# Choosing pages from the first six chunks without a margin in a gated scan with top-1 experts

## The chip, the cores and the metric

The kernel runs on one core of a Trainium2 chip. The metric is device microseconds of one execution; the median of three runs stands for a kernel.

## The reference

```python
def _attn_ref(x, r_gate, i_gate, a_param):          # x: 4 x 5056 x 256
    a_base = sigmoid(a_param)
    a_t = exp(8.0 * sigmoid(r_gate) * log(clip(a_base, 1e-6, 1 - 1e-6)))
    x_gated = sqrt(max(1 - a_t * a_t, 1e-6)) * sigmoid(i_gate) * x
    for t in range(S):
        h = a_t[:, t] * h + x_gated[:, t]
        y[:, t] = h
    return y

def _moe_ref(x, modality_id, w_gate, modality_bias, w1, w2):   # x: 20224 x 256
    logits = x @ w_gate + modality_bias[modality_id]            # 8 experts
    e_idx = argmax(logits); gate_w = softmax(logits)[e_idx]
    for e in range(8):
        mask = e_idx == e
        out[mask] = gate_w[mask] * (relu(x[mask] @ w1[e]) @ w2[e])   # w1: 256x1024, w2: 1024x256
```

A gated linear recurrence runs over 5,056 steps of four sequences; every token of its output goes to one of eight experts and through that expert's two layers. There are two modalities, each with a bias over the experts, and mostly the bias decides: two experts get nearly all tokens.

## The kernel before, in words

**Chunks.** The scan runs over 23 chunks of time steps: four of 128 steps (512 tokens, as there are four sequences), 17 of 256 (1,024 tokens), one of 128 and one of 64. A chunk is loaded, gated and scanned (L513 to L549), scaled and split into two f16 parts (L663, L666), multiplied by the gate weights (L679), and routed (L738 to L806): each token gets its expert and its place behind the tokens that this expert already has. The chunk's tokens are transposed into rows (`rt`) and an indirect DMA of GpSimd scatters them, 128 at a time, into the buffer `rows` in DRAM (L813), which has a region of `NCAP` rows for each expert. Routing also keeps the running count of every expert, `be`, and after chunk c the counts of the two most frequent experts in units of 256 rows, `b2` (L800).

**Pages.** A page is a run of rows of one expert that TensorE takes through both layers. The two frequent experts (`HOT` = 2) have their weights in SBUF throughout, and their pages come in pairs, one for each. `u` holds, in units of 256 rows, where the next page of each begins. `choose_two` (L913 to L929) computes on VectorE the first rows of the next pair (`sel`) and moves `u` on; `load_rows` on SyncE reads `sel` into a register and loads the page as a transposing DMA (`X`, L1091). TensorE does layer 1 (L1166; pages of 512 rows use a scheme with seven products, L1256) and layer 2 (L1326); ScalarE and VectorE evacuate layer 1 (L1103, L1105), ScalarE layer 2 (L1117), and GpSimd scatters 128 output rows at a time (L1121).

**How much may be chosen.** The program is fixed when it is built, while the counts are only known when it runs. So the number and the sizes of the pages are fixed by a planner: when `have` tokens are routed, a pair of `size` rows each is written into the program if `have - 2 * behind(have)` is at least `chosen + 2 * size`, where `behind(n)` = 1.2 sqrt(n) + 8 is a margin for an expert with fewer tokens than half. `enough` gives the time at which the next pair may be chosen. The first pair has 128 rows each, the others 256, and 512 once the sums for the seven products are ready. Where at run time an expert has too few new rows for a page that was planned, its `sel` points at the null page (empty rows), the page is computed for nothing, and `u` stays.

**The end.** After the last chunk the loop stops when the margin allows no further pair; one more pair of 256 is chosen, whose rows may run out (256 empty rows lie behind each expert's last one). Then come two pages of 128 rows that load and convert weights of their own (`cold_weights`: L384 loads 1 MB for each layer into `cr`, L297 takes squares, L285 to L291 make a scale, L347, L350 and L353 convert): `other`, for the rare expert with the most tokens, and `last`, for the expert, frequent or rare, with the most tokens still left. What remains is for a branch:

```python
def more_pages(n, left):
    with tc.If(nc.values_load(tiles["over"], min_val=0, max_val=N) >= 1):
        ...
        add(choose_more(min(n, left)), (0, 4))     # n pages of 128, weights loaded for each
        ...
        if left > n:
            more_pages(3 * n, left - n)
more_pages(2, (N + E * (P - 1)) // P)
```

`over` is the largest number of tokens that an expert has left. The body computes 2 pages of 128 rows, a nested branch 6, the next 18, and so on; each page goes to the expert with the most tokens left, and has its weights loaded and converted as above.

**Order.** The whole program is written by a planner: generators ask for an engine with a duration, and their instructions are emitted in the order of planned times. Waits at run time are by data and buffers. The four `wr` buffers hold the raw and converted weights of one such page; `X` has four buffers, `po` two.

Of the kernel before, what the change touches and what calls it, by code (L numbers as in the profile page):

```python
# [9 lines left out]
F32 = mybir.dt.float32  # L10
# [4 lines left out]
ALU = mybir.AluOpType  # L15
AX = mybir.AxisListType

P = 128
B, S, D, E, FF = 4, 5056, 256, 8, 1024
# [3 lines left out]
WIDE = 512  # L23
NCAP = N + 256
NULLS = E * NCAP
# [4 lines left out]
CHUNKS = [(128 * k, 128) for k in range(4)] + [(512 + 256 * k, 256) for k in range(17)] + [(4864, 128), (4992, 64)]  # L30
# [4 lines left out]
HOT = 2  # L35
# [11 lines left out]
C_STEP = 2  # L47
URGENT = 0.5
HURRY = 5
ROW_STEP = 2.4  # L50
LAG = 3.0


def behind(n):

    return 1.2 * n ** 0.5 + 8


def columns(c):
# [4 lines left out]
def parts(c):  # L64

    return -(-columns(c) // PART)
# [11 lines left out]
def kernel(  # L78
# [13 lines left out]
    nc = tc.nc  # L92
    pool = lambda name, bufs, **k: ctx.enter_context(tc.tile_pool(name=name, bufs=bufs, **k))
    const = pool("const", 1)
    pa = pool("pa", 2)
    sm = pool("sm", 2)
# [30 lines left out]
    for e in range(E):  # L127
# [23 lines left out]
        out=cmp, in0=rank.rearrange("p e o -> p o e").broadcast_to(one8), in1=ids.broadcast_to(one8), op=ALU.is_equal  # L151
# [7 lines left out]

    u = const.tile([1, HOT], F32, name="u")  # L160
    nc.vector.tensor_scalar(out=u, in0=key[:, 0:HOT, 0], scalar1=NCAP / 256.0, scalar2=None, op0=ALU.mult)
    cold = const.tile([1, E], F32, name="cold")
    nc.vector.tensor_scalar(out=cold, in0=ev, scalar1=HOT - 0.5, scalar2=8.0, op0=ALU.is_ge, op1=ALU.mult)

# [16 lines left out]
        out=um1, in_=um1, pattern=[[1, P]], base=0, channel_multiplier=-1,  # L181
# [33 lines left out]
    plan = {"end": 0.0}  # L215
# [474 lines left out]
    def rows_part(c, j):  # L690
# [34 lines left out]
        for u in range(k):  # L725
            yield "POOL", ROW_STEP if c > 7 else 1.3, None
            scatter(f"rows{c}", rt[:, u, 0:ROW], di[:, PART * j + u : PART * j + u + 1])
# [84 lines left out]
    def scatter(group, src, idx):  # L812
        ins = nc.gpsimd.indirect_dma_start(  # L813
            out=rows[:, :], out_offset=bass.IndirectOffsetOnAxis(ap=idx, axis=0),
            in_=src, in_offset=None, bounds_check=NULLS + WIDE - 1, oob_is_err=False,
        ).ins
        for gname in written:
            tc.declare_no_dep(ins, group=gname, reason="every token has a row of its own")
        tc.declare_no_dep(ins, group="loads", reason="a page's rows are written before it is chosen")
        if group not in written:  # L820
            written.append(group)
        puts.append((group, ins.name))
        tc.add_to_no_dep_group(group, ins)
        free["DMA"] = max(free["DMA"], plan["end"] - 1.3) + 0.37
        if "pe" in count:

            tc.add_manual_dep(
                ins, count["pe"], mybir.DependencyInfo(mybir.DependencyClass.Sync, mybir.DependencyReason.DATA)
            )
# [7 lines left out]
    def null_rows():  # L837

        for k in range(2):
# [3 lines left out]
            for e in range(E):  # L843
                yield "POOL", ROW_STEP, None
                scatter("rows_null", nt, ni[:, e : e + 1])
# [13 lines left out]
    pages, queue = [], []  # L859
    count = {"chosen": 0, "ended": False, "cold": 0, "rows": 0}  # L860
# [3 lines left out]
    def routed(t=FAR):  # L864
        n = 0
        while n < NC and all(mark.get(("put", n, j), FAR) <= t for j in range(parts(n))):
            n += 1
        return n

    def enough():  # L870

        at, have = 0.0, 0
        want = count["chosen"] + HOT * (256 if pages else P)
        for c in range(NC):
            at = max([at] + [mark.get(("put", c, j), FAR) for j in range(parts(c))])
            if at >= FAR:
                return FAR
            have += B * CHUNKS[c][1]
            if have - HOT * behind(have) >= want:
                return at  # L880
        return at

    def new_page(size, e, sel, col, late):
        pg = Page()
        pg.size, pg.st, pg.e, pg.sel, pg.col, pg.routed, pg.late = size, size, e, sel, col, routed(plan["end"]), late
        return pg
# [8 lines left out]
    def new_sel():  # L895
        n = count["sel"] = count.get("sel", 0) + 1
        ticket = take("sel")
        return sm.tile([1, 2], I32, name=f"sel{n}", tag="sel", bufs=BUFS["sel"]), ticket
# [4 lines left out]
        if not left:  # L903
            give("sel", ticket)

    def choose_two(size, full):

        sel, ticket = new_sel()
        b2 = tiles["b2", routed(plan["end"]) - 1]
        z = size / 256  # L910
        if full:
            d = sm.tile([1, HOT], F32, name=f"d{len(pages)}", tag="d2")
            nc.vector.tensor_tensor(out=d, in0=b2, in1=u, op=ALU.subtract)  # L913
            yield "DVE", 0.08, None, 0.0
            nc.vector.tensor_scalar(out=d, in0=d, scalar1=z, scalar2=float(NULLS), op0=ALU.is_lt, op1=ALU.mult)
            yield "DVE", 0.08, None, 0.0
            nc.vector.scalar_tensor_tensor(out=sel, in0=u, scalar=256.0, in1=d, op0=ALU.mult, op1=ALU.max)
            first = plan["end"]
            yield "DVE", 0.08, None, 0.0
            if z == 1:  # L920
                nc.vector.scalar_tensor_tensor(out=u, in0=d, scalar=0.0, in1=u, op0=ALU.is_equal, op1=ALU.add)
            else:
                nc.vector.tensor_scalar(out=d, in0=d, scalar1=0.0, scalar2=z, op0=ALU.is_equal, op1=ALU.mult)
                yield "DVE", 0.08, None, 0.0
                nc.vector.tensor_tensor(out=u, in0=u, in1=d, op=ALU.add)
        else:
            nc.vector.tensor_scalar(out=sel, in0=u, scalar1=256.0, scalar2=None, op0=ALU.mult)
            yield "DVE", 0.08, None, 0.0
            nc.vector.scalar_tensor_tensor(out=u, in0=u, scalar=z, in1=b2, op0=ALU.add, op1=ALU.min)  # L929
        left = [0] * HOT  # L930
        for e in range(HOT):
            pg = new_page(size, e, sel, e, not full)
            pg.ticket = ticket, left
            queue_page(pg)
        count["chosen"] += HOT * size
# [51 lines left out]
    def choose_pages():  # L987
        other, at = None, FAR
        summed = lambda: max(mark.get(("sw", e), FAR) for e in range(HOT))
        look = lambda: drained(count["chosen"] - (LOOK if summed() >= FAR else LOOK_END))()  # L990
        while True:
            yield "DVE", 0.08, allof(enough, room("sel"), look)
            if other is None and routed(plan["end"]) == NC:

                add(null_rows(), (0, 5), plan["end"])
                other, at = (yield from choose_cold(True)), len(pages) + 2 * HOT
                add(cold_weights(other), (1, 3), plan["end"])
                yield "DVE", 0.08, room("sel")
            if len(pages) >= at:
                queue_page(other)  # L1000
                at = FAR
            have = sum(B * t for _, t in CHUNKS[: routed(plan["end"])])
            size = 256 if pages else P
            if summed() <= plan["end"] and have - HOT * behind(have) >= count["chosen"] + HOT * WIDE:
                size = WIDE
            if have - HOT * behind(have) < count["chosen"] + HOT * size:
                break
            yield from choose_two(size, True)
        yield "DVE", 0.08, allof(room("sel"), look, seen("null"))
        yield from choose_two(256, False)  # L1010
        if at < FAR:
            queue_page(other)

        t = sm.tile([1, HOT, E], F32, name="thot", tag="thot", bufs=1)
        yield "DVE", 0.08, None, 0.0
        for r in range(HOT):
            nc.vector.tensor_scalar(out=t[:, r], in0=hm[:, r], scalar1=u[:, r : r + 1], scalar2=65536.0, op0=ALU.mult, op1=ALU.mult)
        for r in range(HOT):
            nc.vector.tensor_tensor(out=tk, in0=tk, in1=t[:, r], op=ALU.max)

        yield "DVE", 0.08, room("sel")
        last = yield from choose_cold(False)
        queue_page(last)
        add(cold_weights(last), (1, 3), plan["end"])
        tiles["over"] = over()
        count["ended"] = True
# [342 lines left out]
    def start_chunk(c):  # L1369
        at = PRIO.get(c, (9 + C_STEP * c, 10 + C_STEP * c, 11 + C_STEP * c, 10 + C_STEP * c))  # L1370
        add(load_chunk(c), (0, 10 + C_STEP * c))
        add(scan_chunk(c), (0, at[2]), urgent=c < HURRY)
        add(size_chunk(c), (0, at[2]), urgent=c < HURRY)
        add(split_chunk(c), (0, at[1]), urgent=c < HURRY)
        add(route_chunk(c), (0, at[0]), urgent=c < HURRY)
        for j in range(parts(c)):
            add(rows_part(c, j), (1, at[3]), urgent=c < HURRY)

# [83 lines left out]
```

## Time and profile before

| | |
|---|---|
| median of three runs | 952.21 us (950.91 to 956.86) |
| the profiled execution | 952.39 us, its span 950.5 us |
| mean granted TensorE clock | 0.978 |
| TensorE, matmul | 869.7 us busy, 8,462 instructions |
| VectorE | 700.0 us |
| ScalarE | 671.6 us |
| GpSimd | 484.7 us |

Engines are PE (TensorE; PEld its weight loads, PEq its sequencer), DVE (VectorE), ACT (ScalarE), POOL (GpSimd) and SP (SyncE); a q behind the name is the engine's queue of instructions that aren't counted as busy. A row of a group names the line, engine, operation, tiles and shapes, the count, then busy us and mean ns of one, and idle time before it with what ended it. In the timeline and the chain the first number is the start in us from the span's beginning, the second the duration. In the slices each digit is the busy share of 1/40 of the span in tenths.

### The profile page before, as it was taken

The page shows a single profiled execution, that of the slowest core. Times are in us where ns is not written, and L with a number is a line of the kernel's source. Part 1 is how long each engine was busy: PE and PEld are TensorE (multiplying, and loading weights), DVE is VectorE, ACT ScalarE, POOL GpSimd, SP SyncE. Part 2 cuts the span into 40 slices and gives each one's busy share as a digit, 9 for nine tenths or more (in the row PEclk, how much of TensorE's full clock was granted, in tenths as well). Part 3 has the DMA queues.
Part 4 walks back from the last instruction along what each step waited for, and adds up shares of the span by engine and source line. Part 5 has one row for each costly group of instructions (what it writes and reads, how often), then busy time and mean ns, then how long its engine had stood idle before and what let it go on. Part 6 is the DMA issues. An engine that isn't in the chain of part 4 may idle for free.

```text
span 950.5 us, 22224 instructions
## 1 busy us (share of the span) xinstructions
PE 869.7 (91%) x8462; PEld 775.0 (82%) x8462; DVE 700.0 (74%) x1535; ACT 671.6 (71%) x960; POOL 484.7 (51%) x506
## 2 busy tenths in 40 slices
PE   2268995879999999999999999999999999999996
PEld 1256884769898888888888888988888888888886
DVE  4977785788888877799886888976886666645551
ACT  6876795866898778889578789844765555554742
POOL 5232456367876758857776658745544221222122
PEclk9988997989999999999999999999999999999999
DMA  8746896759999799987788988685733322213410
GB/s 292 230 150 175 223 244 166 223 135 221 267 203 228 226 256 232 265 224 195 185 217 185 274 208 214 163 161 119 184 79 85 57 62 51 52 45 68 131 36 24
DMA packets 222759, 160.43 MB, mean 169 GB/s; under 512 B 197297, under 2 KB 201522, under 8 KB 216114
## 3 DMA queue, kind: packets, MB, share of 16 engines
q1 hardware_dynamic: 205714, 114.49, 51.2%
q0 software_dynamic: 16224, 44.25, 14.2%
q8 instruction: 68, 1.11, 0.5%
q14 instruction: 49, 0.40, 0.1%
q10 hardware_dynamic: 704, 0.18, 0.1%
HBM read 72.96 MB, written 44.48 MB: 124 GB/s over the span
## 4 chain that ended last, share of the span: by engine, by line
PE 46%; issue 21%; DVE 11%; DMA 8%; POOL 7%; ACT 6%; POOLq 0%; SPq 0%; ACTq 0%; DVEq 0%
PE po L1326 21%; PE ph L1166 21%; POOL out_dram L1121 5%; DMA rows<-rt,di 3%; DVE x L546 3%; DVE H L1105 2%; DMA X<-rows 2%; DMA rt<-a 2%; POOL rows L813 1%; PE pb L1256 1%; DVE x L531 1%; ACT H L1103 1%; PE psl L679 1%; PE pa L1256 1%; DVE g L517 1%
## 5 line engine op out<-in xcount | busy, mean ns | idle before, releaser
L1166 PE MATMUL ph<-X,hw 128*128 128x256 f16 (+1 forms) x2688 | 332.1, 276 | 27.3 <-DMA X<-rows 27.3
L1326 PE MATMUL po<-hw,H 128*128 128x256 f16 x2640 | 328.1, 274 | 2.9 <-DVE H L1105 2.7
L1121 POOL DMA_INDIRECT out_dram<-ot,mt x160 | 195.3, 1221 | 259.7 <-ACT ot L1117 217.9
L813 POOL DMA_INDIRECT rows<-rt,di x158 | 229.4, 1452 | 173.3 <-issue 40.7
L1166 PEld LDWEIGHTS <-hw 128*128 128x128 f16 x2688 | 261.3, 100 | 59.5 <-DMA X<-rows 21.3
L1326 PEld LDWEIGHTS <-H 128*128 128x128 f16 x2688 | 259.5, 98 | 35.0 <-DVE H L1105 3.5
L1105 DVE SCALAR_TENSOR_TENSOR H<-ph,H 128x512 f16<-128x512 f32 (+1 forms) x232 | 151.8, 665 | 80.0 <-ACT H L1103 79.6
L1103 ACT ACTIVATE H<-ph 128x512 f16<-128x512 f32 (+1 forms) x232 | 133.2, 578 | 99.9 <-PE ph L1166 88.1
L1117 ACT ACTIVATE ot<-po,gt 128x256 f32<-128x256 f32 x160 | 75.2, 471 | 50.5 <-PE po L1326 43.5
L546 DVE TENSOR_TENSOR_SCAN x<-a,x 128x2048 f32<-128x2048 f32 (+2 forms) x23 | 88.1, 3829 | 0.8
L1326 PE MATMUL po<-hw,Hx 128*128 128x256 f16 x576 | 81.8, 273 | 0.1
L1326 PE MATMUL po<-hw,Hg 128*128 128x256 f16 x576 | 80.2, 273 | 0.0
L1326 PEld LDWEIGHTS <-Hx 128*128 128x128 f16 x576 | 56.2, 98 | 6.7 <-issue 0.3
L1326 PEld LDWEIGHTS <-Hg 128*128 128x128 f16 x576 | 56.4, 98 | 6.5
L1256 PEld LDWEIGHTS <-sw 128*128 128x128 f16 x576 | 56.4, 98 | 6.5
L531 DVE TENSOR_TENSOR x<-g,x 128x2048 f32<-128x2048 f32 (+2 forms) x23 | 45.8, 1991 | 15.8 <-ACT x L529 15.8
L663 ACT ACTIVATE a<-x,scy 128x1024 f16<-128x1024 f32 (+2 forms) x46 | 45.8, 1021 | 12.3 <-DVE scy L289 12.3
L666 DVE SCALAR_TENSOR_TENSOR a<-x,scy,a 128x1024 f16<-128x1024 f32 (+2 forms) x46 | 50.8, 1122 | 1.7 <-ACT a L663 1.7
L522 ACT ACTIVATE a<-a,ch 128x1024 f32<-128x1024 f32 (+2 forms) x46 | 50.7, 1118 | 0.0
L1103 ACT ACTIVATE Hg<-sv 128x512 f16<-128x512 f32 x48 | 30.0, 627 | 26.5 <-DVE sv L1204 26.2
L517 DVE SCALAR_TENSOR_TENSOR g<-g,x 128x2048 f32<-128x2048 f32 (+2 forms) x23 | 45.6, 1984 | 2.9 <-ACT g L513 2.9
L1199 ACT ACTIVATE sv<-pb 128x512 f32<-128x512 f32 x48 | 28.6, 595 | 25.9 <-PE pb L1256 24.3
(210 smaller groups left out, 1109.2 us busy)
## 6 DMA issues: line engine op xcount, KB each, us to landing
a<-in_r_gate_dram SPq DMA_DIRECT2D x17, 1024.0 KB
g<-in_i_gate_dram SPq DMA_DIRECT2D x17, 1024.0 KB
x<-in_x_dram SPq DMA_DIRECT2D x17, 1024.0 KB
wr<-in_moe_w_dram SPq DMA_DIRECT2D x4, 1024.0 KB
cr<-in_moe_w_dram SPq DMA_DIRECT2D x4, 1024.0 KB
a<-in_r_gate_dram SPq DMA_DIRECT2D x5, 512.0 KB
g<-in_i_gate_dram SPq DMA_DIRECT2D x5, 512.0 KB
x<-in_x_dram SPq DMA_DIRECT2D x5, 512.0 KB
```

Of the source, the lines that this page charges most:

```text
L517: nc.vector.scalar_tensor_tensor(out=g, in0=g, scalar=1.0, in1=x, op0=ALU.add, op1=ALU.mult)
L531: nc.vector.tensor_tensor(out=y, in0=g, in1=y, op=ALU.mult)
L546: nc.vector.tensor_tensor_scan(out=y, data0=a, data1=y, initial=0.0, op0=ALU.mult, op1=ALU.add)
L666: nc.vector.scalar_tensor_tensor(out=ys[:, 1, :, u, :], in0=yg[:, :, u, :], scalar=sc, in1=ys[:, 0, :, u, :], op0=ALU.mult, op1=ALU.subtract,)
L813: ins = nc.gpsimd.indirect_dma_start(out=rows[:, :], out_offset=bass.IndirectOffsetOnAxis(ap=idx, axis=0), in_=src, in_offset=None, bounds ...
L1103: nc.scalar.activation(hi, src, AF.Relu)
L1105: nc.vector.scalar_tensor_tensor(out=lo, in0=src, scalar=0.0, in1=hi, op0=ALU.max, op1=ALU.subtract)
L1117: nc.scalar.activation(ot, po, AF.Copy, scale=t.gt[:, a : a + 1])
L1121: ins = nc.gpsimd.indirect_dma_start(out=out[:, :], out_offset=bass.IndirectOffsetOnAxis(ap=t.mt[:, a, 0:1], axis=0), in_=ot, in_offset=No ...
L1166: ins = nc.tensor.matmul(ph[:, v, 0:st], lhsT, rhs, start=(m == 0 and v == 0), stop=(m == len(mm) - 1), skip_group_check=True,)
L1256: ins = nc.tensor.matmul(to[:, v, :], lhsT[s], rhs[x], start=(i in (1, 7) and v == 0 and m == 0), stop=(m == 2), skip_group_check=True,)
L1326: ins = nc.tensor.matmul(prev.po, prev.h(hx, f, rs_), wv[:, wx, f], start=(prev.count == 1), stop=(prev.count == 3 * NF))
```

## The change

For the first six chunks the margin becomes zero. The first pair has 256 rows each like the others, so that the planned sizes add up to all routed tokens after each of these chunks. `choose_two` gets a third form for them: with `u0` the first row of an expert's region, a page begins at `u` or, if fewer than 256 rows lie behind `u`, at `b2 - 1`, 256 rows before the last routed one, and so takes rows that an earlier page had. If the expert has fewer than 256 rows in all, its page is the null page. `u` moves on by one page, but not past `b2`, and doesn't move for a null page. After the sixth chunk the margin and the old forms hold as before.

```diff
+EARLY = 6
-def behind(n):
-    return 1.2 * n ** 0.5 + 8
+def behind(n, c):
+    return 1.2 * n ** 0.5 + 8 if c >= EARLY else 0

+    u0 = const.tile([1, HOT], F32, name="uo")
+    nc.vector.tensor_copy(u0, u)

     def enough():
-        want = count["chosen"] + HOT * (256 if pages else P)
+        want = count["chosen"] + HOT * 256
...
-            if have - HOT * behind(have) >= want:
+            if have - HOT * behind(have, c) >= want:

-    def choose_two(size, full):
+    def choose_two(size, full, again=False):
...
-        if full:
+        if again:
+            d = sm.tile([1, 4, HOT], F32, name=f"d{len(pages)}", tag="d2")
+            nc.vector.tensor_tensor(out=d[:, 0], in0=b2, in1=u0, op=ALU.subtract)
+            nc.vector.scalar_tensor_tensor(out=d[:, 1], in0=b2, scalar=-z, in1=u, op0=ALU.add, op1=ALU.min)
+            nc.vector.tensor_scalar(out=d[:, 2], in0=d[:, 0], scalar1=z, scalar2=float(NULLS), op0=ALU.is_lt, op1=ALU.mult)
+            nc.vector.scalar_tensor_tensor(out=sel, in0=d[:, 1], scalar=256.0, in1=d[:, 2], op0=ALU.mult, op1=ALU.max)
+            nc.vector.tensor_scalar(out=d[:, 3], in0=d[:, 0], scalar1=z, scalar2=z, op0=ALU.is_ge, op1=ALU.mult)
+            nc.vector.tensor_tensor(out=d[:, 3], in0=d[:, 3], in1=u, op=ALU.add)
+            nc.vector.tensor_tensor(out=u, in0=d[:, 3], in1=b2, op=ALU.min)
+        elif full:
             d = sm.tile([1, HOT], F32, name=f"d{len(pages)}", tag="d2")

     def choose_pages():
...
-            size = 256 if pages else P
-            if summed() <= plan["end"] and have - HOT * behind(have) >= count["chosen"] + HOT * WIDE:
+            size = 256
+            if summed() <= plan["end"] and have - HOT * behind(have, n - 1) >= count["chosen"] + HOT * WIDE:
                 size = WIDE
-            if have - HOT * behind(have) < count["chosen"] + HOT * size:
+            if have - HOT * behind(have, n - 1) < count["chosen"] + HOT * size:
                 break
-            yield from choose_two(size, True)
+            yield from choose_two(size, True, n <= EARLY)
```

More of the change, by code (lines that the diff above doesn't have):

```diff
@@ L910, in choose_two @@
         z = size / 256
-        if full:
+        if again:
+            d = sm.tile([1, 4, HOT], F32, name=f"d{len(pages)}", tag="d2")
+            nc.vector.tensor_tensor(out=d[:, 0], in0=b2, in1=u0, op=ALU.subtract)
+            yield "DVE", 0.16, None, 0.0
+            nc.vector.scalar_tensor_tensor(out=d[:, 1], in0=b2, scalar=-z, in1=u, op0=ALU.add, op1=ALU.min)
+            yield "DVE", 0.16, None, 0.0
+            nc.vector.tensor_scalar(out=d[:, 2], in0=d[:, 0], scalar1=z, scalar2=float(NULLS), op0=ALU.is_lt, op1=ALU.mult)
+            yield "DVE", 0.16, None, 0.0
+            nc.vector.scalar_tensor_tensor(out=sel, in0=d[:, 1], scalar=256.0, in1=d[:, 2], op0=ALU.mult, op1=ALU.max)
+            yield "DVE", 0.16, None, 0.0
+            nc.vector.tensor_scalar(out=d[:, 3], in0=d[:, 0], scalar1=z, scalar2=z, op0=ALU.is_ge, op1=ALU.mult)
+            yield "DVE", 0.16, None, 0.0
+            nc.vector.tensor_tensor(out=d[:, 3], in0=d[:, 3], in1=u, op=ALU.add)
+            yield "DVE", 0.16, None, 0.0
+            nc.vector.tensor_tensor(out=u, in0=d[:, 3], in1=b2, op=ALU.min)
+        elif full:
             d = sm.tile([1, HOT], F32, name=f"d{len(pages)}", tag="d2")
@@ L1001, in choose_pages @@
                 at = FAR
-            have = sum(B * t for _, t in CHUNKS[: routed(plan["end"])])
-            size = 256 if pages else P
-            if summed() <= plan["end"] and have - HOT * behind(have) >= count["chosen"] + HOT * WIDE:
+            n = routed(plan["end"])
+            have = sum(B * t for _, t in CHUNKS[:n])
+            size = 256
+            if summed() <= plan["end"] and have - HOT * behind(have, n - 1) >= count["chosen"] + HOT * WIDE:
                 size = WIDE
-            if have - HOT * behind(have) < count["chosen"] + HOT * size:
+            if have - HOT * behind(have, n - 1) < count["chosen"] + HOT * size:
                 break
-            yield from choose_two(size, True)
+            yield from choose_two(size, True, n <= EARLY)
         yield "DVE", 0.08, allof(room("sel"), look, seen("null"))
```

## The prediction

> **What bounds the kernel now.** I read the page first: its span, its shares of busy time and its slices.
>
> ```profile
> span 950.5 us, 22224 instructions
> PE 869.7 (91%) x8462; PEld 775.0 (82%) x8462; DVE 700.0 (74%) x1535; ACT 671.6 (71%) x960; POOL 484.7 (51%) x506
> ...
> PE   2268995879999999999999999999999999999996
> ...
> L1121 POOL DMA_INDIRECT out_dram<-ot,mt x160 | 195.3, 1221 | 259.7 <-ACT ot L1117 217.9
> ```
>
> TensorE is full from the tenth slice on; only in the first nine does it wait for routed tokens. The last row counts the pages: 160 scatters of 128 output rows are 20,480 slots for 20,224 tokens. Next, the busy time by stretch.
>
> ```profile
> core 0: us, PE busy (x) PEld busy (x) DVE busy (x) ACT busy (x) POOL busy (x), PEclk, DMA share, GB/s
> 195.00:215.00 20.00, 13.53 (x108) 11.12 (x107) 15.60 (x37) 12.23 (x18) 11.01 (x9) 0.83 0.52 131
> 215.00:235.00 20.00, 20.00 (x214) 18.02 (x213) 15.54 (x30) 12.08 (x18) 16.95 (x11) 1.00 1.18 240
> ```
>
> The last starvation ends just before 215 us. From there the end is set by how many page slots are left, and by whatever comes after the last planned page. The chain that ended last tells which chunk the last wait was for, and what a group of twelve 256-column matmuls costs.
>
> ```profile
> 201.52 3.84 DMA rows<-rt,di
> 205.43 4.21 DMA X<-rows
> 209.68 2.74 PE ph L1166 x12
> 212.43 1.78 PE po L1326 x12
> 214.21 1.31 PE ph L1166 x12
> ```
>
> It was chunk 5 (the sixth): its last row scatter, its page load, then matmuls. After the wait twelve matmuls take 2.74 and 1.78 us, later 1.31. A 256 page has eight such groups, 10.5 us, and a pair 21.0.
>
> **The gain: 512 slots.** Once chunk 5 is routed, chosen slots go from 3,840 to 4,096. The plan takes one 128 pair first before the change and only multiples of 512 after it.
>
> ```profile
> L915 DVE TENSOR_SCALAR d<-d 1x2 f32<-1x2 f32 x33 | 5.6, 170 | 0.8
> L921 DVE SCALAR_TENSOR_TENSOR u<-d,u 1x2 f32<-1x2 f32 x26 | 4.0, 155 | 0.9
> L923 DVE TENSOR_SCALAR d<-d 1x2 f32<-1x2 f32 x7 | 1.5, 209 | 0.3
> ```
>
> These are the choices of before: 33, of them 26 of 256 and seven others (one of 128, six of 512). So 26x512 + 256 + 6x1024 = 19,712 slots, and 512 in the closing pair make 20,224. The loop stops when 20,224 - 2x178.65 = 19,866.7 is under chosen + 512. In multiples of 512 it stops at 19,456, and the closing pair makes 19,968: 9,984 per frequent expert instead of 10,112. Before chunk 5's pages start, the new kernel has done 3,072 of its 19,968, the old one 2,816 of 19,712+512. So 512 slots fewer are left (16,896 against 17,408 frequent slots, and two 128 pages on either side): 21.0 us.
>
> ```profile
> L1103 ACT ACTIVATE H<-ph 128x512 f16<-128x512 f32 (+1 forms) x232 | 133.2, 578 | 99.9 <-PE ph L1166 88.1
> ```
>
> Of this I give back 3: the 256 slots more in the starved stretch bring four such evacuations (0.58) and two of layer 2, about 3 us on ScalarE, ahead of routing. After chunk 6 the new kernel has only one pair to choose, not two; is TensorE starved again?
>
> ```profile
> 253.60 2.56 POOL L813 DMA_INDIRECT rows<-rt,di  x1 [0.30 <-issue]
> 281.35 1.45 POOL L813 DMA_INDIRECT rows<-rt,di  x1 [1.44 <-PE ph L1166]
> ```
>
> Chunks 7 and 8 are in DRAM at 256.2 and 282.8. The new kernel would run chunk 5's two pairs to 209.7 + 42 = 252 and chunk 6's pair to 273, and with 4.2 us for the load chunk 7's pages can begin at 260. So it isn't, and the gain of **18 us** (none to 21) should last to the end of the planned pages.
>
> **The price: tokens that no planned page takes.** Here the profile isn't enough: I evaluated the reference's router on its inputs as drawn by default. The frequent experts get 10,051 (A) and 10,124 (B) tokens, one other expert 49. Before: slots 10,112 each, B keeps 12, the last page (any expert) takes them, the page for rare experts takes the 49, nothing is left. That agrees with the 160 scatters. After: A and B have 20,175 tokens for 19,968 slots and one page of 128, so at least 79 are left, and the run-time branch at L1401, which before skips its body, is entered.
>
> How many are left depends on the first choice. The first chunk gives A 267 tokens and B 245. The new code gives B the null page when b2 - u0 is below 256, and leaves its u where it was.
>
> ```profile
> 31.52 0.16 DVE L800 TENSOR_REDUCE b<-bh 1x2 f32<-1x16 f32 x1
> 41.58 0.19 DVE L913 TENSOR_TENSOR d<-b,u 1x2 f32<-1x2 f32 x1
> 57.61 0.16 DVE L800 TENSOR_REDUCE b<-bh 1x2 f32<-1x16 f32 x1
> ```
>
> The first choice (41.6) lies between the counts of chunk 0 (31.5) and chunk 1 (57.6): it sees 245. So a whole page of B is lost, and a page moves u by 256 at most, so it never catches up. B's u ends at 9,984 - 256 = 9,728 with 396 left; A ends at 9,984 with 67 left. The last page takes 128 of B (268 left). The branch chooses two pages, both B (140, then 12 left). 67 of A remain, so the nested branch runs too; its **six** pages are written out, and all run: A's 67, B's 12 and four empty ones. That is eight extra pages of 128, each loading and converting 2 MB of weights. What one costs, from the last page of before:
>
> ```profile
> 897.34 1.90 ACT L297 ACTIVATE cw<-cr 128x2048 bf16<-128x2048 f32 x1
> 899.14 0.19 ACT L297 ACTIVATION_READ_ACCUMULATOR cw<-cr 128x1 f32 x1
> ...
> 899.80 0.28 PE L301 MATMUL ptc<-ssc,onesf 128*128 128x1 f32 x2
> ...
> 902.09 1.15 ACT L347 ACTIVATE cw<-cr,csc 128x1024 f16<-128x1024 f32 x1
> ...
> 912.52 0.15 DVE L285 TENSOR_SCALAR csc<-ptc 128x1 int32<-128x1 int32 x1
> ...
> 913.74 1.28 DVE L353 SCALAR_TENSOR_TENSOR cw<-cr,csc,cw 128x1024 f16<-128x1024 f32 x1
> 914.94 0.75 DVE L350 TENSOR_SCALAR cw<-cr,csc 128x1024 f16<-128x1024 f32 x1
> ...
> 917.78 0.15 DVE L463 TENSOR_TENSOR pinv<-civ,civ 128x1 f32<-128x1 f32 x1
> ...
> 939.41 0.42 DVE L1105 SCALAR_TENSOR_TENSOR H<-ph,H 128x256 f16<-128x256 f32 x1 [1.56 <-ACT H L1103]
> 939.75 0.20 DVE L1313 TENSOR_SCALAR gt<-mt,pinv 128x1 f32<-128x1 f32 x1
> 940.10 2.78 PE L1326 MATMUL po<-cw,H 128*128 128x256 f16 x24
> 942.97 0.47 ACT L1117 ACTIVATE ot<-po,gt 128x256 f32<-128x256 f32 x1 [2.19 <-PE po L1326]
> ```
>
> Beside other work the conversion took 897.34 to 917.93, 20.6 us. Alone, its instructions give: first square 2.1, TensorE's sum with the waits around it 0.75 (899.33 to 900.08), three scale-bit steps from 912.52 on 0.55, two halves on ScalarE 2.4; then the second square (ScalarE goes in order) 2.1, 0.75 and 0.55 again, and on VectorE 2x(0.75+1.28) = 4.1, and `pinv` with its wait 0.3: 13.6 us. VectorE's four layer-1 tails (0.42 each) lie among it, 1.7. Layer 2, 24 matmuls, is 2.78 at full clock; after a wait the chain above shows 2.74 and 1.78 for a group of 1.31, so I put 4.2. Its evacuation, 0.8 with the wait, stands on ScalarE ahead of the next page's square. Layer 1 hides under the conversion, and the next page's weight load too, since its raw buffers come free at conversion. A page in sequence costs 13.6 + 1.7 + 4.2 + 0.8 = **20.3 us** (13.6 if pages overlap fully; 27 if each load waits for the page before).
>
> The Trainium skill's page "TensorE: Matmul & The Clock Gate" (Part 1) says that after an idle window the array runs at half clock until it has been busy for some 3.4 us. This trace agrees (2.74 against 1.31 after a wait); if the gate stayed open from layer 1 on, the page would cost 18.9, and the sum would be 10 us less.
>
> A page that begins a branch cannot be prepared ahead, since VectorE chooses it after its last work of the page before. Rows for that:
>
> ```profile
> L1401 DVEq TENSOR_LOAD <-over x1: 546/546/546, 939.4 to 939.4; - x1
> L1401 PEldq COMPARE_BRANCH  x1: 4194/4194/4194, 941.4 to 941.4; - x1
> 785.04 0.15 DVE L940 TENSOR_TENSOR k<-be,tk 1x8 f32<-1x8 f32 x1
> ...
> 786.25 0.16 DVE L971 CAST sel<-sf 1x2 int32<-1x2 f32 x1
> 8.48 1.60 SPq L384 DMA_DIRECT2D wr<-in_moe_w_dram  x2
> 13.62 1.14 PE L317 MATMUL pt<-wr 128*128 128x128 bf16 x9 [5.29 <-DMA wr<-in_moe_w_dram]
> ```
>
> Register load and branch 0.7, choosing until sel is written 1.4, SyncE's read and issue about 1.1 (an estimate), the first megabyte 5.1 (8.48 to 13.62): 8.3, then 13.6 + 1.7 + 4.2. That is 27.8 from VectorE's last work to the end of layer 2. The 4.2 us on TensorE's queue is the jump past the body; it is in the tail of before already. Entering a body, I take at nothing (up to 4.2 for each of two).
>
> **The sum.** Planned pages end on TensorE at 942.9 - 18 = 925; VectorE is done 3 us earlier. The first extra page ends at 925 - 3 + 27.8 = 949.8, the second at 970.1. VectorE is free 4.2 earlier, so the third ends at 965.9 + 27.8 = 993.7, and five more at 20.3 give 1095.2. From the last matmul to the end of the span before took 950.5 - 942.9 = 7.6: span 1102.8. The profiled execution took 952.39 for its 950.5, so 1.9 lies around: **1104.7, say 1105 us**. That execution stands 0.2 from the median of 952.21, so nothing is to be shifted. Choosing adds four VectorE instructions of some 0.15 us in each of eight choices, under 5 us, off the path while VectorE has gaps.
>
> **Rivals.**
> *Two extra pages* (about 980): if the first pair were chosen with chunk 1's counts, B would have 495 there, its page would start at its own first row, and later ones would lap by up to 50 rows. It then keeps 190, 62 after the last page, and two pages take these and A's 67: 970.1 + 7.6 + 1.9 = 980. Against it stand 31.5, 41.6 and 57.6 above, and a plan that chooses as soon as the chunk's rows are put. 8 in 100.
> *None* (about 934, faster): the only faster outcome. The branch would have to stay shut, so that 952.4 - 18 is left. It decides at 20,096 tokens on the frequent experts (19,968 + 128); the drawn ones are 20,175. It needs other inputs, on which the 160 scatters say only that before its own limit held. 5 in 100.
> *A third level* of eighteen pages: 1105 + 18x20.3 + 7.5 = 1478, if lost rows exceeded eight pages; the counts don't give it. 3 in 100.
> *The change doesn't do what it says*: that is in the forecast, for B's 245 first tokens aren't handed on at once, a null page is.
>
> The Trainium skill's page "Runtime: NRT & Kernel Launch" (Instruction fetch mechanics) says that a taken branch out of the fetched window stalls for a fetch. The 4.19 us above fits; if the bodies were reached by such jumps, the time would be 8 us more.
>
> **How the numbers follow.** Eight extra pages have 84 in 100. Their own bounds: pages that overlap fully, 6x6.7 = 40 less, and an open clock gate, 10 less, with 3 more of gain, give about 1052; conversion at the 20.6 seen beside other work (8x7 = 56 more), or loads in sequence (6x6.7 = 40), two fetches (8), or no gain (18), not all at once, about 1165. I set 1052 to 1165, which leaves the other cases (16 in 100) and a few in 100 of the main one out. A measurement of this kernel tells about 1% from no change. Faster by over 1%: 0.05; within 1%: 0.02 (no extra page, and no gain); slower: 0.93.
>
> **What would show it.** In the profile after: 158 + 8 = 166 scatters at L1121's statement; 32 choices instead of 33, eight of them in the new form; weight loads `cr` 20 instead of 4; a gap-ridden TensorE for the last 170 us, with groups of 36 matmuls or so between conversions, and ScalarE, VectorE in turn on the chain; planned pages ending near 925. Wrong it would be if the scatters are 158 or 160, if pages follow each other every 13 or every 27 us, or if the planned pages end at 943 or later.

## The result, and the profile after

The changed kernel takes **1076.05 us** (median, 1075.65 to 1076.14) against 952.88: a ratio of 1.129 (95% interval 1.125 to 1.132). Forecast were 1105 and 1052 to 1165. The profiled execution has a span of 1074.3. The kernel before took 967 to 970 us beside some of the runs below and 953 beside the others, so each time there stands beside that of the kernel before.

From the page after: span, slices of TensorE and its clock, output scatters; and from the groups by line the squares of page weights (x20), the choices in the new (x8) and in the old form (x25), and those of the latter that take 512 rows (x5).

```profile
span 1074.3 us, 23769 instructions
PE   2389979999999999999999999999999999334454
PEclk9999989999999999999999999999999999666767
L1141 POOL DMA_INDIRECT out_dram<-ot,mt x166 | 215.3, 1297 | 385.2 <-ACT ot L1137 322.1 <-DVE mk L976 23.3 <-issue 19.4
L300 ACT ACTIVATE cw<-cr 128x2048 bf16<-128x2048 f32 x20 | 38.0, 1900 | 24.5 <-DMA cr<-in_moe_w_dram 24.5
L917 DVE TENSOR_TENSOR d<-b,uo 1x2 f32<-1x2 f32 x8 | 1.4, 181 | 0.0
L932 DVE TENSOR_TENSOR d<-b,u 1x2 f32<-1x2 f32 x25 | 3.6, 145 | 0.1
L942 DVE TENSOR_SCALAR d<-d 1x2 f32<-1x2 f32 x5 | 1.1, 211 | 0.2
```

The scatters are 166, so 158 + 8; two squares a page and two planned pages leave eight extra ones. The choices are 8 + 25 = 33 and not the forecast 32: only five pairs have 512 rows, where the kernel before has six. In the last six slices TensorE is busy for 3 to 5 tenths at 6 to 7 tenths of its clock: these are the extra pages. One by one, in the timeline after (start, duration): the last planned page's layer 2 (911.38), then for each extra page layer 2 (`po<-cw`), the first square of its weights (`cw<-cr`) and some of the loads (`cr`).

```profile
911.38 2.78 PE L1346 MATMUL po<-cw,H 128*128 128x256 f16 x24
913.95 0.16 DVE L990 CAST sel<-sf 1x2 int32<-1x2 f32 x1
917.74 0.37 SPq L387 DMA_DIRECT2D cr<-in_moe_w_dram  x1
922.77 1.91 ACT L300 ACTIVATE cw<-cr 128x2048 bf16<-128x2048 f32 x1 [8.04 <-DMA cr<-in_moe_w_dram]
935.62 3.20 PE L1346 MATMUL po<-cw,H 128*128 128x256 f16 x24
939.23 1.90 ACT L300 ACTIVATE cw<-cr 128x2048 bf16<-128x2048 f32 x1
951.87 2.58 PE L1346 MATMUL po<-cw,H 128*128 128x256 f16 x22 [0.49 <-DVE H L1125]
962.85 1.91 ACT L300 ACTIVATE cw<-cr 128x2048 bf16<-128x2048 f32 x1 [7.89 <-DMA cr<-in_moe_w_dram]
975.05 1.24 SPq L1111 DMA_TRANSPOSE X<-rows  x1
975.70 2.57 PE L1346 MATMUL po<-cw,H 128*128 128x256 f16 x22 [0.46 <-DVE H L1125]
977.76 1.02 SPq L387 DMA_DIRECT2D cr<-in_moe_w_dram  x2
983.06 1.91 ACT L300 ACTIVATE cw<-cr 128x2048 bf16<-128x2048 f32 x1 [4.28 <-DMA cr<-in_moe_w_dram]
995.40 1.23 SPq L1111 DMA_TRANSPOSE X<-rows  x1
995.92 2.58 PE L1346 MATMUL po<-cw,H 128*128 128x256 f16 x22 [0.33 <-DVE H L1125]
1016.13 2.58 PE L1346 MATMUL po<-cw,H 128*128 128x256 f16 x22 [0.21 <-DVE H L1125]
1031.67 2.97 PE L1346 MATMUL po<-cw,H 128*128 128x256 f16 x24
1035.05 1.90 ACT L300 ACTIVATE cw<-cr 128x2048 bf16<-128x2048 f32 x1
1047.69 2.58 PE L1346 MATMUL po<-cw,H 128*128 128x256 f16 x22 [0.60 <-DVE H L1125]
1050.67 1.90 ACT L300 ACTIVATE cw<-cr 128x2048 bf16<-128x2048 f32 x1
1063.12 2.97 PE L1346 MATMUL po<-cw,H 128*128 128x256 f16 x24
```

The planned pages end at 914.2, not 942.9: **28.7 us earlier**. The extra pages end at 938.8, 954.5, 978.3, 998.5, 1018.7, 1034.6, 1050.3 and 1066.1: **151.9 us** for eight. Their spacing has three sizes. A page whose weights were loaded ahead takes 15.6 to 15.9 (the second and the last three). The fourth and the fifth take 20.2: the fourth's square waits 4.28 us for a load issued only at 977.76, the fifth's 4.27. The pages that begin a branch take 24.7 and 23.8.

The starved stretch and the rest, before and after (columns: us, busy us and count on PE, PEld, DVE, ACT and POOL, then clock, DMA share, GB/s):

```profile
0.00:300.00 300.00, 229.14 (x2229) 200.89 (x2230) 231.70 (x536) 232.23 (x295) 161.21 (x216) 0.94 0.81 214
300.00:943.00 643.00, 640.57 (x6235) 574.07 (x6233) 468.32 (x999) 438.92 (x666) 322.51 (x289) 1.00 0.60 149
```

```profile
0.00:300.00 300.00, 243.82 (x2384) 213.62 (x2385) 240.49 (x571) 241.69 (x305) 176.58 (x229) 0.98 0.83 222
300.00:914.20 614.20, 611.81 (x5959) 548.73 (x5956) 447.74 (x968) 415.24 (x629) 309.39 (x275) 1.00 0.60 151
```

Of the 28.7 us, 14.7 are idle time of TensorE that went in the first 300 us, and 14.1 are less busy time (869.7 against 855.6). The granted clock in those 300 us rose from 0.94 to 0.98.

### The profile page after: what moved, and what is told of

Its sections match the earlier page's. It is cut to its first block, busy times and chain, and to the rows that moved or that the text cites. A ratio compares the mean times of both kernels' runs of the same rounds, so it can differ in the third digit from the quotient of the medians.

```text
span 1074.3 us, 23769 instructions
## 1 busy us (share of the span) xinstructions
PE 923.9 (86%) x8948; PEld 823.9 (77%) x8948; DVE 769.4 (72%) x1764; ACT 721.7 (67%) x1022; POOL 494.7 (46%) x512
## 4 chain that ended last, share of the span: by engine, by line
PE 62%; issue 13%; DVE 10%; ACT 9%; DMA 4%; POOL 1%; SPq 1%; POOLq 0%; ACTq 0%; DVEq 0%
PE po L1346 31%; PE ph L1186 21%; PE pb L1276 4%; DVE x L549 3%; PE pc L1276 2%; PE pa L1276 2%; DVE H L1125 2%; ACT H L1123 1%; PE psl L682 1%; DVE g L520 1%; ACT x L532 1%; ACT a L666 1%; DMA rt<-a 1%; ACT cw L300 1%; DMA rows<-rt,di 1%
## 5 line engine op out<-in xcount | busy, mean ns | idle before, releaser
L1141 POOL DMA_INDIRECT out_dram<-ot,mt x166 | 215.3, 1297 | 385.2 <-ACT ot L1137 322.1
L1186 PE MATMUL ph<-X,hw 128*128 128x256 f16 x2784 | 343.8, 274 | 15.5 <-DMA X<-rows 15.3
L1346 PE MATMUL po<-hw,H 128*128 128x256 f16 x2784 | 343.9, 274 | 2.7 <-DVE H L1125 0.9
L1346 PEld LDWEIGHTS <-H 128*128 128x128 f16 x3024 | 292.0, 98 | 42.4 <-DVE H L1125 5.4
L1125 DVE SCALAR_TENSOR_TENSOR H<-ph,H 128x512 f16<-128x512 f32 (+1 forms) x272 | 170.6, 644 | 92.2 <-ACT H L1123 91.6
L1123 ACT ACTIVATE H<-ph 128x512 f16<-128x512 f32 (+1 forms) x272 | 150.9, 560 | 116.8 <-PE ph L1186 113.0
L1346 PE MATMUL po<-hw,Hx 128*128 128x256 f16 x480 | 68.4, 273 | 1.2 <-ACT ot L1137 0.7
L1346 PE MATMUL po<-hw,Hg 128*128 128x256 f16 x480 | 67.0, 273 | 0.0
L356 DVE SCALAR_TENSOR_TENSOR cw<-cr,csc,cw 128x1024 f16<-128x1024 f32 x40 | 50.6, 1282 | 12.5 <-ACT cw L350 12.0
L300 ACT ACTIVATE cw<-cr 128x2048 bf16<-128x2048 f32 x20 | 38.0, 1900 | 24.5 <-DMA cr<-in_moe_w_dram 24.5
```

Of the source, the lines that this page charges most:

```text
L356: nc.vector.scalar_tensor_tensor(out=lo, in0=src, scalar=sc, in1=hi, op0=ALU.mult, op1=ALU.subtract)
L1123: nc.scalar.activation(hi, src, AF.Relu)
L1125: nc.vector.scalar_tensor_tensor(out=lo, in0=src, scalar=0.0, in1=hi, op0=ALU.max, op1=ALU.subtract)
L1141: ins = nc.gpsimd.indirect_dma_start(out=out[:, :], out_offset=bass.IndirectOffsetOnAxis(ap=t.mt[:, a, 0:1], axis=0), in_=ot, in_offset=No ...
L1186: ins = nc.tensor.matmul(ph[:, v, 0:st], lhsT, rhs, start=(m == 0 and v == 0), stop=(m == len(mm) - 1), skip_group_check=True,)
L1346: ins = nc.tensor.matmul(prev.po, prev.h(hx, f, rs_), wv[:, wx, f], start=(prev.count == 1), stop=(prev.count == 3 * NF))
```

## The experiments

Where two kernels were run beside different runs of the kernel before, I compare ratios, or distances within one trace. `shut`, `nest2`, `two_small`, `after_again` and `rows_late` are one execution each.

**shut**: the planned pages alone.

```diff
-        with tc.If(nc.values_load(tiles["over"], min_val=0, max_val=N) >= 1):
+        with tc.If(nc.values_load(tiles["over"], min_val=0, max_val=N) >= N):
```

> The branch's condition is never met, so the tokens that no planned page takes stay without an output. Theory (the planned pages end 28.7 us earlier and the eight extra pages cost the rest): the changed kernel's last planned matmul ends at 914.2, its tail from the last matmul is 8.2 and 1.8 lies around, so 924 us (920 to 930). Rival (the extra pages' instructions cost something already while the planned pages run, by the order on SyncE or by branches): more, 935 to 950.

944.5 us, beside 969.6: 25 less than before, where the theory has 29 (924 against 953). The time itself misses the expected 920 to 930 and lies in the rival's range, and so the ends of the planned pages decide, here and in `nest2`, which was run beside it and does compute extra pages:

```profile
932.57 2.78 PE L1346 MATMUL po<-cw,H 128*128 128x256 f16 x24
```

They end at 935.4 here, without any extra page, and at 931.3 in `nest2` (the first line below). Extra pages that run don't make the planned ones later, so the rival falls. One execution leaves some us open, but the 123 us of loss are gone, and a gain stands in their place.

**nest2**: four extra pages instead of eight.

```diff
-                more_pages(3 * n, left - n)
+                more_pages(n, left - n)
```

> The nested branch has two pages instead of six, so four of the eight extra pages, the empty ones, are gone. Theory: the fourth extra page ends at 998.5 in the changed kernel, so 998.5 + 8.2 + 1.8 = 1009 us (1004 to 1015). Rival (entering a branch is what costs, not the page): two entries as before, so 1060 or more.

1021.1 us beside 969.6, above the expected 1004 to 1015. Layer 2 of the last planned page and of the four extra ones in its timeline:

```profile
928.53 2.78 PE L1346 MATMUL po<-cw,H 128*128 128x256 f16 x24
952.93 2.58 PE L1346 MATMUL po<-cw,H 128*128 128x256 f16 x22 [0.52 <-DVE H L1125]
968.46 2.88 PE L1346 MATMUL po<-cw,H 128*128 128x256 f16 x24
992.39 2.92 PE L1346 MATMUL po<-cw,H 128*128 128x256 f16 x24
1008.27 3.22 PE L1346 MATMUL po<-cw,H 128*128 128x256 f16 x24
```

From 931.3 to 1011.5 four pages take 80.2 us, against 84.3 in the changed kernel, where the fourth waits for its weights. So what is above the expected time came with the planned pages, which end at 931.3 and not at 914.2. The four empty pages are the rest; entering a branch is not what costs most.

**two_small**: no null page. The first chunk gives two pairs of 128 rows, and a page that may lap waits for the scatters of the two pages before it.

```diff
-        want = count["chosen"] + HOT * 256
+        want = count["chosen"] + HOT * (256 if len(pages) >= 2 * HOT else P)
...
-            size = 256
+            size = 256 if len(pages) >= 2 * HOT else P
...
+        laps = [f"outs{t.pg.e}_{t.pg.k - d}" for d in (1, 2)] if t.pg.again else []
...
```

> Chunk 0 gives two pairs of 128 rows instead of one of 256 (pages that lap wait for the scatter of the page before, to keep two writes of a row apart). Theory (expert B's null page costs six of the eight extra pages): B's second page laps by 11 rows, no null page, B keeps 190 and A 67, so two extra pages; the second ends at 954.5 in the changed kernel, 954.5 + 8.2 + 1.8 = 964 us (957 to 973). Rival (the eight pages come from the shorter plan, whatever the first choice): 1070 to 1080.

975.5 us beside 969.6, 2.5 above the expected range, and again the planned pages end later (925.5 against 914.2). Its timeline has just two extra pages, 40.6 us from 925.5 to 966.2 (the first two of the changed kernel took 40.3):

```profile
922.76 2.78 PE L1352 MATMUL po<-cw,H 128*128 128x256 f16 x24
947.83 2.58 PE L1352 MATMUL po<-cw,H 128*128 128x256 f16 x22 [0.39 <-DVE H L1125]
963.37 2.79 PE L1352 MATMUL po<-cw,H 128*128 128x256 f16 x24
```

So B's null page in the first choice is what turns two extra pages into eight: 245 tokens where 256 were needed cost six pages.

**two_small_close**: the same, and a closing pair of 128 more, which takes what the branch took.

```diff
         yield from choose_two(256, False)
+        yield "DVE", 0.08, allof(room("sel"), look)
+        yield from choose_two(P, False)
```

> As the kernel with two small pairs, and one more closing pair of 128 rows. Theory: nothing is left for the branch; planned pages end at 914.2 + 10.5, and 8.2 + 1.8 behind, so 935 us, 0.98 of before (0.975 to 0.99). Rival (what the early choice gains is only the 256 slots that the shorter plan lacks, and they are back here): 950 to 955, no change.

954.9 beside 969.6: 0.985 (0.980 to 0.990), within the expected ratio. It is 10.4 us over `shut`, with a pair worth 10.5; as `shut` is one execution and the six of this kernel lie between 947.5 and 961.2, so close a match is luck. Again as **two_small_close2**:

> The kernel with two small pairs and one more closing pair, on this chip. Theory (planned pages of the changed kernel plus 10.5 us for the pair, no branch): 914.5 + 10.5 + 8.2 + 1.8 = 935 us, ratio 0.98. Rival (two pairs of 128 in the first chunk lose again what one of 256 gained): 945 or more, as the kernel with a small first pair.

952.4 beside 967.3, 0.985 (0.981 to 0.989). This version is 1.5% faster than the kernel before, both times. The 935 isn't reached, and the rival's "945 or more" is; but both are meant beside 953, of which they are 0.981 and 0.992. The measured ratio lies nearer to the first and below the second; the first run's rival, no change, is out.

**after_again** and **rows_late**: why the fourth and the fifth extra page are late. In the branch, a page's row load is written behind its own weights' conversion:

```diff
+            if after_weights:
+                yield "SP", 0.0, seen(("cw", pg.c)), 0.0
...
-            add(load_rows(first), (1, 2))
+            add(load_rows(first, True), (1, 2))
```

> The changed kernel as it is, on the chip of the two runs beside it, to compare them with. Both theories: 1076 us, or some 1.5% more if this chip is as slow as the one of the runs before it.

> In the branch a page's rows are loaded only after its weights are converted, so SyncE's queue no longer holds a row load that waits for an X buffer ahead of the next page's weight loads. Theory (extra pages 4 and 5 cost 20.2 us instead of 15.8 because their weight loads stand behind such a row load): 4.4 us less on each of the two, 9 us less than the changed kernel beside it (6 to 11). Rival (the weights are late because their buffers are): no difference, within 2 us.

1077.0 and 1062.9: 14 us less, more than the 6 to 11 expected. Layer 2 of pages 3 to 6 in the kernel with late rows:

```profile
970.99 2.96 PE L1348 MATMUL po<-cw,H 128*128 128x256 f16 x24
987.00 2.58 PE L1348 MATMUL po<-cw,H 128*128 128x256 f16 x22 [0.62 <-DVE H L1127]
1002.42 2.99 PE L1348 MATMUL po<-cw,H 128*128 128x256 f16 x24
1018.38 3.15 PE L1348 MATMUL po<-cw,H 128*128 128x256 f16 x24
```

Pages 4 and 5 now follow after 15.6 and 15.8. So what held their weights in SyncE's queue were the loads of the seventh and the eighth page's rows (975.05 and 995.40 above), which are issued when layer 1 of pages 3 and 4 has ended (975.02 and 995.37) and an `X` buffer is free. The remaining 5 us are at the two branch entries, where the first weight load no longer stands behind the rows: 21.7 and 21.7 from the end of the page before instead of 24.0 and 24.2 in `after_again`. I hadn't counted that.

**first_small**: everything of the change but the first pair's size.

```diff
-        want = count["chosen"] + HOT * 256
+        want = count["chosen"] + HOT * (256 if pages else P)
...
-            size = 256
+            size = 256 if pages else P
```

> The margin and the new form as in the change, but the first pair has 128 rows as before, so the planner chooses the same number of slots after every chunk as before and the branch stays shut. Theory (gain and loss both come from the first pair's size by way of the multiples of 512): the time of before, ratio 1.00 (0.99 to 1.01). Rival (the form with laps and its four more VectorE instructions, or choosing without a margin, moves the time by itself): off by more than 1%.

945.3 beside 953.0: 0.9925 (0.990 to 0.995). There are the same slots as before and no extra page, so the loss does come from the first pair's size. But the time isn't quite that of before. Its last planned matmul and its first 300 us:

```profile
931.07 2.78 PE L1346 MATMUL po<-cw,H 128*128 128x256 f16 x24
0.00:300.00 300.00, 233.66 (x2329) 205.61 (x2330) 236.99 (x572) 239.03 (x302) 173.19 (x223) 0.95 0.83 222
```

The planned pages end at 933.9, 9.0 before those of the kernel before; by the medians it is 7.7 (this is the fastest of five executions). From there to the changed kernel's 914.2 are 19.7, and 18.7 to the 915.1 of `after_again`, which ran beside it: this is about what the first pair's size gains. The 0.75% also means that about half of the 1.5% of `two_small_close` may be there without choosing more in the first chunk.

**order_only**: is the 9 us a matter of the written order? The kernel before, with only the planner's durations of the early choices changed.

```diff
-            yield "DVE", 0.08, None, 0.0
+            early = routed(plan["end"]) <= 6
+            for _ in range(4 if early else 1):
+                yield "DVE", 0.16 if early else 0.08, None, 0.0
...
```

> The kernel before, instruction for instruction, but the planner is told that a choice within the first six chunks takes six steps of 0.16 us, as the new form does; so only the written order of the instructions may differ. Theory (the kernel with a small first pair came out 8 us under before because the planner wrote the early chunks in another order): about 945 us, ratio 0.99. Rival (the new form itself, or choosing without a margin, gives the 8 us): ratio 1.00.

975.6 beside 967.3: 1.007 (1.004 to 1.011), slower. The theory fell in this form. The edit also did more than it was meant to, as the choices show (all, and those that aren't of 256 rows):

```profile
L917 DVE TENSOR_SCALAR d<-d 1x2 f32<-1x2 f32 x34 | 6.1, 180 | 0.5
L925 DVE TENSOR_SCALAR d<-d 1x2 f32<-1x2 f32 x6 | 1.1, 183 | 0.2
```

The kernel before has 33 and seven. So not only the written order changed: the planner made two pairs of 256 of one of 512. The slots are the same, but a page of 512 rows has 180 matmuls (2,160 for twelve in the kernel before) and two of 256 have 192, so that 24 matmuls more are needed for the pair; at 1.31 us for twelve, I estimate 2.6 of the 8.3 us for that. The run doesn't separate the rest. What an order alone is worth isn't shown, then, nor whether the 0.75% of `first_small`, whose order differs too, come from its order or from the new form.

## Why the prediction was right, point by point

**The count of extra pages** was right: eight, for the reason given, and `two_small`, `nest2` and `shut` each take their part of it away. None of the three rivals came. With the counts worked out, the changed kernel never even uses its laps: in the first six chunks A has 265 or more new rows at every choice, and B, after its null page, 462 or more. The new form's laps are dead code on these inputs, and its null page does the harm.

**The sum** came out 28.7 us over, 1104.7 against 1076.05 (that the planned pages, too, end 28.7 earlier is a coincidence). Its terms:

| term | forecast | measured |
|---|---|---|
| planned pages end | 925 (gain 18) | 914.2 (gain 28.7) |
| entry to the first extra page's end, from VectorE's last work | 27.8 | 26.4 (912.4 to 938.8) |
| the same for the nested branch | 27.8 | 25.4 (952.9 to 978.3) |
| a page in sequence | 20.3, six times | 15.6 to 15.9 four times, 20.2 twice |
| last matmul to the end | 7.6 | 8.2 |

Nearly all of the 28.7 is the gain (10.7) and four of the pages in sequence (18.2 together). That two others did take the forecast 20.3 is luck, as told below.

**The gain** was sized 18: 21.0 for 512 slots less 3 that I gave back. The 21.0 took it for granted that six pairs of 512 rows stay. With five, as the 33 choices show, the 24 matmuls more take 2.6 us back (an estimate, at 1.31 for twelve), so the slots that the new plan saves are worth 18.4, and from `first_small`, which has six such pairs, to the changed kernel the traces have 18.7 to 19.7. The orders of these two differ as well, so the match to an us proves little; the 3 us given back aren't seen. What the sum lacked is the 9.0 (7.7 by the medians) that came with the new form even without the larger pair; their cause stays open. I had also taken the row load of chunk 5 as the last starvation. In the changed kernel TensorE waits once more, 2.3 us before 221.6, for VectorE's part in routing chunk 7, and the second pair of chunk 5 stands behind that. The new form has three VectorE instructions more than the old one for 256 rows, not four.

**The page in sequence** was mis-sized where its weights were ahead. From a first square to the next it is 15.6 to 15.9 for the last pages (1035.05 to 1050.67, for one). The end of a conversion on VectorE, on the second extra page:

```profile
951.33 0.15 DVE L466 TENSOR_TENSOR pinv<-civ,civ 128x1 f32<-128x1 f32 x1
951.39 0.75 DVE L1125 SCALAR_TENSOR_TENSOR H<-ph,H 128x256 f16<-128x256 f32 x2
952.18 0.74 DVE L1125 SCALAR_TENSOR_TENSOR H<-ph,H 128x256 f16<-128x256 f32 x2
```

The conversion takes 12.2 (939.23 to `pinv`'s end at 951.5), not 13.6: its second square begins 5.0 after the first, not 5.8, and what follows takes 7.3, not 7.8. VectorE's four layer-1 tails, for which I added 1.7 within the conversion, come behind `pinv`: layer 2 waits 0.49 for the first two, and the other two run beside its matmuls. Layer 2 takes 2.6 to 3.2, not 4.2, and from its end to the next square it is 0.4, not 0.8.

The Trainium skill's page "TensorE: Matmul & The Clock Gate" (Part 1) has an idle window bring the array back to half clock until it has been busy for a while. The trace agrees, with a granted clock of 0.69 over the extra pages, but layer 1 pays it. Its groups by line, before (two pages) and after (ten), for 48 matmuls a page:

```profile
L1166 PE MATMUL ph<-X,cw 128*128 128x128 f16 x96 | 6.7, 219 | 0.0
L1186 PE MATMUL ph<-X,cw 128*128 128x128 f16 x480 | 44.3, 279 | 0.0
```

That is 3.35 us a page before, and (44.3 - 6.7)/8 = 4.7 on an extra page, while layer 2, right behind it, is nearly at full rate; and layer 1 ends within half an us of the conversion, so that it costs next to nothing. My 4.2 priced layer 2 like the first matmuls behind a wait, 4.56 us in the row that I took it from. On an extra page these are layer 1's, behind a wait of 4.61. (For a gate that stays open I took off 10 us; eight times 1.4 would be 11.)

**The weight loads** were called hidden, and for two of six pages they weren't. I had seen that the raw buffers come free at conversion, but not that a row load ahead of them in SyncE's queue waits for an `X` buffer; `rows_late` shows that. It made the forecast's 20.3 right for these two pages for a wrong reason. The first page of a branch has such a load ahead, too: from `sel` (written at 914.1) to the issue of the weights (917.74) it is 3.6 us, where I had put 1.1 for SyncE, an estimate that no row gave. It came out near 27.8 in all, as conversion and layer 2 took 16.1 there (922.77 to 938.82) and not 19.5.

**The branch.** The register loads and jumps of the changed kernel:

```profile
L1421 DVEq TENSOR_LOAD <-over x3: 308/309/553, 912.0 to 1063.8; - x3
L1421 PEldq COMPARE_BRANCH  x4: 64/142/3415, 913.1 to 1068.8; - x4
```

Entering a body costs TensorE's queue 0.09 us the first time and 0.06 the second; only the jump past the third body takes 3.4. To take the entries at nothing was right, and the 8 us more that jumps into the bodies would have cost didn't come.

## What to carry to other kernels

Where a static plan is filled at run time, count what every planned slot gets before asking what an early start gains: here 256 slots dropped from the end and one page wasted at the start sent 335 tokens into a fallback that costs 16 to 25 us for each 128 rows, against 5.3 us for each 128 of a planned pair. A margin that looks like waste pays for a cheap path; if it is taken away, put a slot for the shortfall at the end, as the closing pair of 128 does for 10.5 us, once no page is wasted. And a load in a queue that is in order is only as early as the one ahead: a prefetch shouldn't stand behind a load that waits for a buffer, which here cost 14 us.

## What the runs showed that I had not expected

An edit meant to change only the durations that the planner assumes also changed its plan: one pair of 512 rows became two of 256, and the time moved by 0.7%. The change itself did so as well, by the same pair. So before two kernels written by such a planner are compared, their choices and pages of each size should be counted, and a gain or a loss under 1% between them says little about the edit.
